# Float32 products of the attention, 64 output rows at a time on two halves of the TensorE array

## The chip, the cores and the metric

The kernel runs on one core of a Trainium2 chip. The metric is the device time of one execution in microseconds (us), taken from the first to the last work of the program. The kernel before takes 977.47 us, the median of three runs that lie between 977.23 and 977.64 us.

## The reference

A linear attention with random features (4 batches, 8 heads, 576 rows of 64 columns, 128 features), and behind it two feed-forward blocks of 512 x 2048 x 512 on the 2304 rows that come out:

```python
def phi(x):
    proj = np.einsum('bhsd,md->bhsm', x, omega)
    h = proj - np.sum(x * x, axis=-1, keepdims=True) / 2.0
    h = h - np.max(h, axis=-1, keepdims=True)
    return np.exp(h) / np.sqrt(m)
q_p, k_p = (phi(q_s), phi(k_s))              # q and k, scaled
kv = np.einsum('bhsm,bhsd->bhmd', k_p, v)
z = np.sum(k_p, axis=2)
num = np.einsum('bhsm,bhmd->bhsd', q_p, kv)
den = np.einsum('bhsm,bhm->bhs', q_p, z)[..., None] + 1e-06
x = num / den                                # then rows (b, s), columns (h, d)
x = relu(x @ w_in) ** 2 @ w_out              # first block
x = elu(x @ w_in2) @ w_out2                  # second block
```

The change touches the two products `kv` (phi(k) with v; a column of ones in v gives `z` in the same product) and `num` (phi(q) with `kv`, which gives `den` in its last column).

## The kernel before, in words

The 576 rows of a head are 4 blocks of 128 and 64 left over. A unit of work is a pair of heads of one batch, for k or for q (`(b, "k", hp)`, `(b, "q", hp)`), and one unit `(b, "l", 0)` holds the left-over rows of all eight heads. That makes 9 units a batch and 36 in all. A loop written out by hand runs over the units with `stages`, a table of steps and of the delay of each: squares, transposes (`transposed`, tile `pt`, line 275), projection with omega in three float32r products (`projected`, `pp`, line 292), maxima, exponentials (`featured`, `ph`, line 321), and then the steps that matter here, all in plain float32:

- `used`, for a k unit: for each of two heads, four products add phi(k) of a block, transposed by the product itself, times `v` of that block (128 rows by 65 columns) into `pk` (line 340). A ninth product adds the left-over rows of both heads (130 columns, line 344). ScalarE then copies `pk` to `kv` (line 348).
- `used`, for a q unit: transposes phi(q) to `qT` (tile `pq`, line 358).
- `attended`, for a q unit: for each of two heads, four products of a 128 x 128 block of `qT` with `kv` (65 columns) into `pn` (line 381). After every second pair of heads, four products for the left-over rows, which have 64 output rows only (`pl`, line 398). VectorE divides by the last column.
- `turned`: transposes the result for the feed-forward blocks (`px`, line 413, and `pxl`, line 422).

Each of the nine or eight products holds one operand in the array (the weights: phi(k) or `qT`, 128 rows by 128 columns) and streams the other (`v` or `kv`). A float32 product stands as two weight loads and two matmuls in the trace. The order of the instructions on TensorE is the order in which this loop issues them; `used` of a k unit and `attended` of the q unit before it stand right behind one another. In the last units, the first steps of the feed-forward blocks (`gemm1`, line 457; `gemm2`, line 508) are interleaved, and they fill the rest of the program.

Of the kernel before, what the change touches and what calls it, by code (L numbers as in the profile page):

```python
# [17 lines left out]
def linear_attention_two_ffn_kernel(  # L18
# [12 lines left out]
    nc = tc.nc  # L31
    P = 128
    B, H, S, D = q.shape
# [4 lines left out]
    C = S // P  # L38
# [10 lines left out]
    SCALE = float(D) ** -0.25  # L49
    HALF = 0.5 * SCALE * SCALE  # L50
    EPS = 1e-6 * M

    REBIAS = 2.0 ** -112
    assert LH * L == P and C == 4 and H == 4 * LH and 2 * NP * (C * P) == W * H and NP == KD
# [9 lines left out]
    def page(shape, name, dt=F32):  # L64
        return pages.tile([P] + list(shape), dt, tag="page", name=name)

    def psum(name):
        return ps.tile([P, W], F32, tag="bank", name=name)

    def flat(t):  # L70
        return t.rearrange("p a b -> p (a b)")
# [134 lines left out]
    st = {}  # L206
# [120 lines left out]
    def used(u):  # L327

        b, kind, hp = u
        nm = f"{b}{kind}{hp}"  # L330
        phs = st[u]["ph"]
        if kind == "k":
            ll = st[b, "l", 0]
            kv = sp.tile([P, 2, D + 1], F32, tag="kv", name=f"kv{nm}")
            pk = psum(f"pk{nm}")

            for h in range(2):
                o = pk[:, h * (D + 1):(h + 1) * (D + 1)]
                for c in range(C):
                    nc.tensor.matmul(  # L340
                        o, phs[h][:, c, :], st[u]["v"][:, h * C + c, :], start=h == 0 and c == 0, stop=False,
                        skip_group_check=True,
                    )
            nc.tensor.matmul(
                pk[:, :2 * (D + 1)], ll["ph"][0][:, hp, :], flat(ll["v"][:, 2 * hp:2 * hp + 2, :]),
                start=False, stop=True, skip_group_check=True,
            )
            nc.scalar.copy(out=flat(kv), in_=pk[:, :2 * (D + 1)])
            st[u]["kv"] = kv
            return  # L350
        st[u]["qT"] = []
        for g in range(2):
            if kind == "l" and g == 0:
                continue
            qT = page([4, P], f"qT{nm}_{g}")
            pt = psum(f"pq{nm}_{g}")
            for i in range(4):
                nc.tensor.transpose(pt[:, i * P:(i + 1) * P], phs[g][:, i, :], ident)
            nc.scalar.copy(out=flat(qT), in_=pt)
            st[u]["qT"].append(qT)  # L360

    def normal(pvs, os, w, nm):
        rd = sp.tile([P, 4 * len(pvs), 1], F32, tag="rd", name=f"rd{nm}")
        rds = [rd[:w, 4 * i:4 * i + 4] for i in range(len(pvs))]
        for pv, r in zip(pvs, rds):
            nc.vector.tensor_scalar(out=r, in0=pv[:, :, D:D + 1], scalar1=EPS, scalar2=None, op0=ALU.add)
        nc.vector.reciprocal(out=rd[:w], in_=rd[:w])
        for pv, o, r in zip(pvs, os, rds):
            nc.vector.tensor_tensor(out=o, in0=pv[:, :, :D], in1=r.to_broadcast([w, 4, D]), op=ALU.mult)

    def attended(u):

        b, kind, hp = u
        if kind != "q":
            return
        xs = page([C, 2, D], f"xs{b}_{hp}")
        pvs = []
        for h in range(2):
            pn = psum(f"pn{b}_{hp}_{h}")
            for c in range(C):  # L380
                nc.tensor.matmul(  # L381
                    pn[:, c * (D + 1):(c + 1) * (D + 1)], st[u]["qT"][h][:, c, :], st[b, "k", hp]["kv"][:, h, :],
                    start=True, stop=True,
                )
            pvs.append(pn[:, :C * (D + 1)].rearrange("p (c d) -> p c d", d=D + 1))
        normal(pvs, [xs[:, :, h, :] for h in range(2)], P, f"{b}_{hp}")
        st[u]["xs"] = xs
        if hp % 2 == 0:
            return
        qd = hp // 2  # L390
        if qd == 0:
            st[b, "xs"] = page([H, D], f"xsl{b}")
        xs = st[b, "xs"]
        qTl = st[b, "l", 0]["qT"][0]
        pn = psum(f"pl{b}_{qd}")
        for i in range(4):
            j, h = 2 * qd + i // 2, i % 2
            nc.tensor.matmul(  # L398
                pn[:L, i * (D + 1):(i + 1) * (D + 1)], qTl[:, j, h * L:(h + 1) * L],
                st[b, "k", j]["kv"][:, h, :], start=True, stop=True,  # L400
            )
        normal([pn[:L, :4 * (D + 1)].rearrange("p (c d) -> p c d", d=D + 1)], [xs[:L, 4 * qd:4 * qd + 4, :]], L, f"l{b}_{qd}")
# [151 lines left out]
    def moe_pieces():  # L554
# [14 lines left out]
    stages = (  # L569
        (transposed, 2), ("weights", 0), (featured, 4), ("step", 1), (projected, 3), (load, 0),  # L570
        (maxima, 3), (squared, 1), ("step", 0), (used, 5), (turned, 7), (attended, 6), (load_v, 2),
    )
    DEPTH = max(d for f, d in stages)
# [5 lines left out]
    with tc.manual_schedule():  # L579
# [4 lines left out]
        for s in range(1, len(units) + DEPTH):  # L584
# [21 lines left out]
            u = s - DEPTH  # L606
# [36 lines left out]
```

## Time and profile before

| | |
|---|---|
| time, median of three runs | 977.47 us |
| span of the profiled execution, from the first to the last instruction | 975.3 us |
| what lies around the span in a run, by the difference | 2.2 us |
| TensorE (PE) busy | 968.4 us, 99% |
| TensorE weight loads (PEld) busy, beside the matmuls | 837.1 us, 86% |
| VectorE (DVE) busy | 621.1 us, 64% |
| ScalarE (ACT) busy | 479.2 us, 49% |
| GpSimd (POOL) busy | 91.2 us, 9% |

Busy means that at least one instruction of the engine was recorded as running. A matmul is recorded from its start to the modelled end of its result, so the records of neighbouring matmuls overlap, and a matmul's recorded length (275 ns, say) is not what it takes from the next one. What it takes is read from the distance between starts, or from the chain of work, in which each piece counts up to where the next takes over.

### The profile page before, as it was taken

The numbers are of one execution on the slowest core, as the hardware profiler recorded it, in microseconds if no ns is written. First come the engines' busy times: TensorE is split into PE (matmuls) and PEld (weight loads), VectorE is DVE, ScalarE is ACT, GpSimd is POOL, SyncE is SP. The second block draws the span as 40 slices with busy tenths as digits, with TensorE's granted clock in tenths as the row PEclk, the third lists the DMA queues.
The fourth block names the chain that finished last, engine by engine and source line by source line (L and its number), as shares of the span: only waits on it lengthen the run. The fifth ranks groups of instructions, "written<-read, shape, count | busy, mean of one in ns | idle before, by whom it ended". The sixth has DMA issues, their size and how long they took to land.

```text
span 975.3 us, 14149 instructions
## 1 busy us (share of the span) xinstructions
PE 968.4 (99%) x5457; PEld 837.1 (86%) x5457; DVE 621.1 (64%) x1130; ACT 479.2 (49%) x1052; POOL 91.2 (9%) x196
## 2 busy tenths in 40 slices
PE   9999999999999999999999999999999999999998
PEld 9999999999888888888888888888888888888886
DVE  6888886574584358435764587558745884485444
ACT  6887885442352234223443366446544654454443
POOL 7455553000000000000000000000000000000000
PEclk9999999999999999999999999999999999999999
DMA  9355420020140013001210022003200220000211
GB/s 249 93 144 140 137 66 2 1 87 1 43 130 1 1 48 104 22 1 44 87 43 1 22 85 68 1 1 101 73 1 0 87 87 1 1 22 13 74 44 65
DMA packets 56610, 53.40 MB, mean 55 GB/s; under 512 B 25568, under 2 KB 50144, under 8 KB 56544
## 3 DMA queue, kind: packets, MB, share of 16 engines
q1 hardware_dynamic: 55696, 52.08, 17.7%
q8 instruction: 43, 0.70, 0.3%
q10 hardware_dynamic: 848, 0.43, 0.2%
q14 instruction: 23, 0.19, 0.1%
HBM read 47.78 MB, written 4.72 MB: 54 GB/s over the span
## 4 chain that ended last, share of the span: by engine, by line
PE 97%; DMA 1%; SPq 1%; ACT 1%; DVE 0%; issue 0%; ACTq 0%
PE ph L457 41%; PE py L508 41%; PE pn L381 3%; PE pk3k L340 1%; PE pk2k L340 1%; PE pk1k L340 1%; PE pk0k L340 1%; PE px L413 1%; PE pp3k L292 1%; PE pp1k L292 1%; PE pp3q L292 1%; PE pp0q L292 1%; PE pp1q L292 1%; DMA ld0k<-in_k_dram 1%; PE pl L398 1%; PE pp0k L292 0%
## 5 line engine op out<-in xcount | busy, mean ns | idle before, releaser
L457 PE MATMUL ph<-xh,wh 128*128 128x512 f32 (+1 forms) x688 | 245.7, 357 | 0.0
L457 PE MATMUL ph<-xl,wh 128*128 128x512 f32 (+1 forms) x688 | 245.7, 357 | 0.0
L457 PE MATMUL ph<-xh,wl 128*128 128x512 f32 (+1 forms) x688 | 245.7, 357 | 0.0
L469 ACT ACTIVATE r<-ph 128x512 f32<-128x512 f32 (+1 forms) x92 | 46.8, 509 | 241.1 <-PE ph L457 241.1
L473 DVE TENSOR_TENSOR gf<-r 128x512 f32<-128x512 f32 (+1 forms) x92 | 53.3, 579 | 154.5 <-ACT r L469 154.1
L457 PEld LDWEIGHTS ph<-xh,wh 128*128 128x128 f32 x688 | 129.3, 188 | 21.3 <-DVE gf L483 0.2
L457 PEld LDWEIGHTS ph<-xl,wh 128*128 128x128 f32 x688 | 129.3, 188 | 21.1
L457 PEld LDWEIGHTS ph<-xh,wl 128*128 128x128 f32 x688 | 129.3, 188 | 20.5
L74 DVE TENSOR_TENSOR gl<-gf,gh 128x512 fp32r<-128x512 f32 (+1 forms) x172 | 105.2, 611 | 47.3 <-ACT gh L484 35.5
L508 PE MATMUL py<-gh,wh 128*128 128x512 f32 (+1 forms) x368 | 127.4, 346 | 0.0
L508 PE MATMUL py<-gh,wl 128*128 128x512 f32 (+1 forms) x368 | 126.8, 345 | 0.0
L508 PE MATMUL py<-gl,wh 128*128 128x512 f32 (+1 forms) x368 | 126.7, 344 | 0.0
L482 DVE SCALAR_TENSOR_TENSOR r<-r,t 128x512 f32<-128x512 f32 (+1 forms) x80 | 51.0, 637 | 105.2 <-ACT t L479 105.2
L508 PE MATMUL py<-wh,gh 128*128 128x512 f32 x288 | 113.7, 395 | 0.0
L508 PE MATMUL py<-wh,gl 128*128 128x512 f32 x288 | 113.5, 394 | 0.0
L508 PE MATMUL py<-wl,gh 128*128 128x512 f32 x288 | 113.3, 393 | 0.0
L477 ACT ACTIVATE gf<-ph 128x512 f32<-128x512 f32 (+1 forms) x80 | 44.4, 555 | 93.5 <-PE ph L457 93.3
L484 ACT CAST gh<-gf 128x512 fp32r<-128x512 f32 (+1 forms) x80 | 46.2, 578 | 82.0 <-DVE gf L483 80.4
L508 PEld LDWEIGHTS py<-gh,wh 128*128 128x128 f32 x368 | 69.2, 188 | 9.4
L508 PEld LDWEIGHTS py<-gh,wl 128*128 128x128 f32 x368 | 69.2, 188 | 9.2
L508 PEld LDWEIGHTS py<-gl,wh 128*128 128x128 f32 x368 | 69.2, 188 | 9.0
L531 DVE TENSOR_TENSOR ya<-py,ya 128x512 f32<-128x512 f32 x108 | 67.2, 682 | 0.6 <-PE py L508 0.6
(325 smaller groups left out, 1460.6 us busy)
## 6 DMA issues: line engine op xcount, KB each, us to landing
st<-in_moe_w_in_dram SPq DMA_DIRECT2D x32, 512.0 KB, 3.6
st<-in_moe_w_out_dram SPq DMA_DIRECT2D x32, 512.0 KB, 3.4
vk<-in_v_dram SPq DMA_DIRECT2D x32, 128.0 KB, 4.2
out_dram<-ya SPq DMA_DIRECT2D x16, 256.0 KB, 2.2
ld0k<-in_k_dram SPq DMA_DIRECT2D x4, 256.0 KB, 4.8
ld0q<-in_q_dram SPq DMA_DIRECT2D x4, 256.0 KB, 4.8
ld1k<-in_k_dram SPq DMA_DIRECT2D x4, 256.0 KB, 4.6
ld1q<-in_q_dram SPq DMA_DIRECT2D x4, 256.0 KB, 4.2
```

Source lines behind the costliest of these rows:

```text
L74: eng.tensor_tensor(out=out, in0=whole, in1=hi.bitcast(F32), op=ALU.subtract)
L292: nc.tensor.matmul(pp[:, i * 2 * M:(i + 1) * 2 * M], a[:, cs], o, start=(n == 0), stop=(n == 2))
L340: nc.tensor.matmul(o, phs[h][:, c, :], st[u]["v"][:, h * C + c, :], start=h == 0 and c == 0, stop=False, skip_group_check=True,)
L381: nc.tensor.matmul(pn[:, c * (D + 1):(c + 1) * (D + 1)], st[u]["qT"][h][:, c, :], st[b, "k", hp]["kv"][:, h, :], start=True, stop=True,)
L457: nc.tensor.matmul(ph[:, :n], wt[:, cs], x_part(xt, moe, i, c)[:, n0:n1], start=(m == 0), stop=(m == 3 * KD - 1))
L469: nc.scalar.activation(out=r, in_=ph[:, :n], func=AF.Relu)
L473: nc.vector.tensor_tensor(out=gf, in0=r, in1=r, op=ALU.mult)
L477: nc.scalar.activation(out=gf, in_=ph[:, :n], func=AF.Relu, scale=-1.0)
L482: nc.vector.scalar_tensor_tensor(out=r, in0=r, scalar=1.0, in1=t, op0=ALU.add, op1=ALU.mult)
L484: nc.scalar.copy(out=gh, in_=gf)
L508: nc.tensor.matmul(y, *((w[:, ts], a) if moe == 0 else (a[:, ts], w)), start=j == 0 and m == 0 and t % per == 0, stop=j == GF - 1 and m == ...
L531: nc.vector.tensor_tensor(out=ya_t[i, t], in0=yv, in1=ya_t[i, t], op=ALU.add)
```

## The change

The weights of each product of lines 340, 344 and 381 are cut into two halves of 64 columns, and each half goes out as a product of its own, to output partitions 0 to 63 or 64 to 127 of the same bank. The two halves are issued alternately. What is computed, the buffers and the instructions on the other engines stay. In the built program such a product carries the array tile 128 rows x 64 columns, at column 0 or at column 64; lines 340, 344 and 381 carried 128 x 128 before, and line 398 carried 128 x 64 at column 0 already and still does.

```diff
+    HALVES = (slice(0, P // 2), slice(P // 2, P))
...
             for h in range(2):
-                o = pk[:, h * (D + 1):(h + 1) * (D + 1)]
                 for c in range(C):
-                    nc.tensor.matmul(
-                        o, phs[h][:, c, :], st[u]["v"][:, h * C + c, :], start=h == 0 and c == 0, stop=False,
-                        skip_group_check=True,
-                    )
-            nc.tensor.matmul(
-                pk[:, :2 * (D + 1)], ll["ph"][0][:, hp, :], flat(ll["v"][:, 2 * hp:2 * hp + 2, :]),
-                start=False, stop=True, skip_group_check=True,
-            )
+                    for m in HALVES:
+                        nc.tensor.matmul(
+                            pk[m, h * (D + 1):(h + 1) * (D + 1)], phs[h][:, c, m], st[u]["v"][:, h * C + c, :],
+                            start=h == 0 and c == 0, stop=False, skip_group_check=True,
+                        )
+            for m in HALVES:
+                nc.tensor.matmul(
+                    pk[m, :2 * (D + 1)], ll["ph"][0][:, hp, m], flat(ll["v"][:, 2 * hp:2 * hp + 2, :]),
+                    start=False, stop=True, skip_group_check=True,
+                )
...
             for c in range(C):
-                nc.tensor.matmul(
-                    pn[:, c * (D + 1):(c + 1) * (D + 1)], st[u]["qT"][h][:, c, :], st[b, "k", hp]["kv"][:, h, :],
-                    start=True, stop=True,
-                )
+                for m in HALVES:
+                    nc.tensor.matmul(
+                        pn[m, c * (D + 1):(c + 1) * (D + 1)], st[u]["qT"][h][:, c, m], st[b, "k", hp]["kv"][:, h, :],
+                        start=True, stop=True,
+                    )
```

TensorE's rows at the second k unit of the first batch, before. A row is a line, an operation, output and inputs, and the shape of the output; `pk` comes from `used`, `pn` from `attended` of the q unit before:

```order
L292 MATMUL pp0k_1_435<-oml,th0k_349 128x256
L340 MATMUL pk0k_457<-vk_106,ph0k_0_353 128x65 x4
L340 MATMUL pk0k_457<-vk_106,ph0k_1_358 128x65 x4
L344 MATMUL pk0k_457<-vl_112,ph0l_0_238 128x130
L381 MATMUL pn_0_0_469<-kv0k_276,qT0q_0_391 128x65 x4
L381 MATMUL pn_0_1_474<-kv0k_276,qT0q_1_398 128x65 x4
L275 MATMUL pt0k_485<-ident,ld0k_377 128x128 x4
```

The same place on TensorE in the changed program (its lines have shifted):

```order
L293 MATMUL pp0k_1_444<-oml,th0k_358 128x256
L341 MATMUL pk0k_466<-vk_106,ph0k_0_362 64x65 x8
L341 MATMUL pk0k_466<-vk_106,ph0k_1_367 64x65 x8
L346 MATMUL pk0k_466<-vl_112,ph0l_0_238 64x130 x2
L384 MATMUL pn_0_0_487<-kv0k_276,qT0q_0_400 64x65 x8
L384 MATMUL pn_0_1_496<-kv0k_276,qT0q_1_407 64x65 x8
L276 MATMUL pt0k_511<-ident,ld0k_386 128x128 x4
```

Nothing has moved; each product stands twice with half the output rows, between the same neighbours. There are 17 unbroken stretches of products with the 128 x 64 tile in the changed program, and 8 (those of line 398) in the one before.

## Rows read from the trace of the kernel before

**Rows 1.** The page: span, TensorE's busy time, the chain's shares by engine.

```profile
span 975.3 us, 14149 instructions
...
PE 968.4 (99%) x5457; PEld 837.1 (86%) x5457; DVE 621.1 (64%) x1130; ACT 479.2 (49%) x1052; POOL 91.2 (9%) x196
...
PE 97%; DMA 1%; SPq 1%; ACT 1%; DVE 0%; issue 0%; ACTq 0%
```

**Rows 2.** Chain of work, 10 to 60 us: start, us, what.

```profile
22.18 1.73 PE pk0k L340 x16
23.91 0.28 PE pk0k L344 x2
24.18 1.73 PE pn L381 x16
25.92 0.44 PE pt0k L275 x4
...
32.96 1.73 PE pn L381 x16
34.70 0.61 PE pl L398 x8
35.31 0.59 PE pt1k L275 x4
```

**Rows 3.** Busy time by stretch, instructions in brackets, granted TensorE clock, DMA.

```profile
core 0: us, PE busy (x) PEld busy (x) DVE busy (x) ACT busy (x) POOL busy (x), PEclk, DMA share, GB/s
13.00:33.00 20.00, 20.00 (x180) 20.00 (x178) 15.77 (x32) 19.56 (x64) 14.07 (x31) 1.00 0.84 235
...
13.00:133.00 120.00, 119.66 (x1061) 117.64 (x1059) 101.69 (x225) 102.39 (x322) 68.07 (x141) 1.00 0.49 136
133.00:190.00 57.00, 57.00 (x501) 56.36 (x501) 36.52 (x90) 33.31 (x101) 14.80 (x30) 1.00 0.07 20
```

**Rows 4.** TensorE by line and form: busy us, mean ns, idle before; first batch.

```profile
L381 PE MATMUL pn<-kv0k,qT0q 128*128 128x65 f32 x64 | 7.6, 272 | 0.0
L340 PE MATMUL pk0k<-vk,ph0k 128*128 128x65 f32 x64 | 7.6, 272 | 0.0
L344 PE MATMUL pk0k<-vl,ph0l 128*128 128x130 f32 x8 | 1.8, 302 | 0.0
L398 PE MATMUL pl<-kv0k,qT0l 128*64 128x65 f32 x16 | 1.4, 228 | 0.0
```

**Rows 5.** Weight loads in order of time (start, us, what), three short windows.

```profile
32.69 1.87 PEld L381 LDWEIGHTS pn<-kv0k,qT0q 128*128 128x128 f32 x16
34.62 0.54 PEld L398 LDWEIGHTS pl<-kv0k,qT0l 128*64 128x64 f32 x8
...
25.36 0.41 PEld L381 LDWEIGHTS pn<-kv0k,qT0q 128*128 128x128 f32 x3
```

**Rows 6.** Matmuls in order of time, beside the last row of the group above.

```profile
25.42 0.39 PE L381 MATMUL pn<-kv0k,qT0q 128*128 128x65 f32 x2
```

**Rows 7.** Lines 340 and 381: duration min/median/max, first and last start.

```profile
L340 PE MATMUL pk3k<-vk,ph3k x64: 218/275/275, 129.3 to 177.8; 128*128 128x65 f32 x64
...
L381 PE MATMUL pn<-kv2k,qT2q x64: 221/275/275, 103.7 to 132.9; 128*128 128x65 f32 x64
```

**Rows 8.** ScalarE's waits, 13 to 133 us: total, times, longest.

```profile
ACT th2q L278 <- PE pt2q L275: 3.4, 2, 2.7
ACT th1q L278 <- PE pt1q L275: 2.9, 2, 2.1
ACT th2k L278 <- PE pt2k L275: 2.7, 1, 2.7
...
ACT th0k L278 <- PE pt0k L275: 0.4, 1, 0.4
```

## The prediction, made before the changed kernel was run

> **What bounds the kernel now.** I read the page first: TensorE is busy for 99% of the span and holds 97% of the chain that ended last [rows 1]. The list of TensorE's groups then shows no idle time ahead of the lines that change [rows 4], and by stretches TensorE is busy for 119.66 of the 120 us from 13 to 133 us and for all of the 57 us up to 190 us, at the full granted clock of 1.00, its level of 2.4 GHz [rows 3]. So a nanosecond less on TensorE ends the program a nanosecond earlier, as long as no other engine comes to be late. Two are near in the first stretch: VectorE has 101.69 us of work there and ScalarE 102.39; ScalarE is busy for 19.56 of the 20 us from 13 to 33 us [rows 3]. Behind 133 us both have much room.
>
> What do the changed lines take? Recorded durations overlap, so I take the chain in order of time [rows 2]: the eight products of a k unit take 1.73 us (16 pairs of load and matmul), the ninth 0.28, the eight of a q unit 1.73. There are 16 k units and 16 q units with one such group each (4 batches, 4 pairs of heads): 16 x (1.73 + 0.28 + 1.73) = **59.8 us**, all of it on the path.
>
> What limits such a product? Sixteen loads of 128 columns cover 1.87 us, the last of them 0.19 long by itself, so they start (1.87 - 0.19)/15 = 112 ns apart; the loads of line 398, half as wide and followed by matmuls of the same 65 columns, start (0.54 - 0.14)/7 = 57 ns apart, 0.14 being the length of one of these [rows 5]. Half the columns, half the distance: the pace is set by the weight load, not by the 65 columns that stream. The 130 columns of line 344 take 0.28 for two, hardly more than two of the others, and say the same [rows 2].
>
> **The change part by part.** (a) The 512 pairs of lines 340 and 381 become 1024 with half the load, the 32 pairs of line 344 become 64. What one takes in the new order, with the two halves of the array in turns, no row shows: line 398 uses one half alone. I bound it from both sides. Lowest: the halves work fully side by side, and two pairs take the 57 ns of one in line 398, 28.5 ns each. That gives 1024 x 28.5 ns = 29.2 us and 64 x 57 ns = 3.6 us (twice the columns), 32.8 us. Next: a load starts when the matmul before it has started, but a matmul on a half that stands empty need not wait for its whole load. In line 381 a load starts at 25.36 and its matmul at 25.42, 56 ns into the 112 [rows 5, 6]; at half the width that is 28 ns for the first pair of a half and 57 for the second, 42.5 on average: 43.5 us, and with some 70 ns for the wide ones 4.5 more, 48.0 us. Highest with the overlap missing: 57.5 ns each, as in line 398, which is the first rival.
>
> I take 36 ns, the middle of 28.5 and 42.5, since nothing in the rows chooses between free loads and loads in step: 36.9 us, and 64 x 60 ns = 3.8 us, together **40.7 us**.
>
> The Trainium skill (TensorEngine Tiling (Array Packing), section Key Properties) says that different tiles of the array can execute weight loads and matmuls in parallel. By that alone the sum would be the 32.8 us of the lowest bound; no run here shows it yet.
>
> (b) Entering and leaving the 128 x 64 tile costs something. Line 398 shows it: its eight pairs take 0.61 in the chain where 8 x 57 ns are 0.46, and the transposes behind it take 0.59, where they take 0.44 behind line 381 [rows 2]: 0.15 + 0.15 = 0.30 us for each stretch. There are 17 stretches instead of 8 (the products of a k unit, a q unit and line 398 now share one): 9 x 0.30 = **2.7 us** more.
>
> (c) Nothing else is added: no wait, no DMA, no work on another engine. ScalarE's copy of `pk` and VectorE's first read of `pn` wait for the last of the products as before, and get it earlier if these are faster.
>
> Sum on TensorE: 40.7 + 2.7 - 59.8 = -16.4 us.
>
> (d) How much of it reaches the end? The first three batches and the first k group of the fourth lie before 133 us (line 340 of batch 3 begins at 129.3, line 381 of batch 2 ends at 132.9) [rows 7]: 13 + 12 of 32 groups, so 12.8 of the 16.4 us. The stretch of 120 us would become 107 us, with ScalarE busy for 102.4 and VectorE for 101.7 of them. Of ScalarE's 17.6 us of idle time, 14.6 end with a transpose of TensorE (seven rows from 3.4 down to 0.4) [rows 8], so they do shrink when TensorE is earlier; but at 95% of occupation each jitter costs, and from 13 to 33 us ScalarE has nothing left to give. I count two thirds, 8.5 us. Behind 133 us VectorE and ScalarE have 20 us of room, and the other 3.6 us count whole. Together 12.1 us. The profiled execution's span is 975.3 us, with 2.2 us around it that do not change: 975.3 + 2.2 - 12.1 = **965.4 us**, against the median of 977.47.
>
> The two ends of this case: at 42.5 ns the sum is 48.0 + 2.7 - 59.8 = -9.1 us, of which 7.1 x 2/3 + 2.0 = 6.7 arrive: 970.8 us. At 28.5 ns it is -24.3 us; 19.0 fall before 133 us, and two thirds of these and all of the rest make 18.0: 959.5 us. Were ScalarE's idle time used to the last (17.6 + 5.3), 954.6 us.
>
> **The rivals.** *The halves don't overlap* (the change doesn't do what it says): each half-load waits its turn, 57.5 ns as in line 398. For it speaks that in every stream of this trace the loads come one behind another, at a distance that goes by their columns [rows 5]. Against it, that all these streams use a single tile, so that no load had anywhere else to go. Price: 1024 x 57.5 = 58.9 us, the wide ones 64 x 57.5 = 3.7 us, or 64 x 110 = 7.0 us if the 130 columns now count (a transpose of 128 columns takes 0.44/4 = 110 ns [rows 2]); with 2.7 for the stretches and less 59.8 that is +5.5 to +8.8 us, all on the path: 983 to 986.3 us, **985**. It decides from 52.5 ns a pair on: there 1088 pairs and 2.7 us make the old 59.8.
>
> *The turns hold the loads up*: a load for one half can't start while a matmul of the other still streams. Then at each change of halves the 57 ns of streaming and a load of 28 to 57 stand one behind the other, and the second pair adds 57: 71 to 85 ns a pair, 72.7 to 87 us, with some 6.5 for the wide ones and 2.7 for the stretches +22 to +36 us: 1000 to 1014 us. The even pace of line 398, where a load runs beside the matmul of its own tile [rows 5], speaks against it. The Trainium skill (TensorE: Matmul & The Clock Gate, Part 3, The mechanism) has the rule behind it: loads overlap with matmuls in flight only when the row group differs, and two column halves share all rows. Line 398 already breaks that rule in its own tile.
>
> *The gain is swallowed*: TensorE saves as forecast, but ScalarE and VectorE make the first 133 us as long as before, by their own order of work. Then only the last 7 of 32 groups count, 2 to 5 us: 972 to 975.5 us. The 14.6 us of idle time that TensorE ends speak against it.
>
> *A pace close to break-even*, 50 to 54 ns, would end within 2 us of before.
>
> **How the numbers follow.** Overlap with a gain that arrives (954.6 to 970.8): 0.52. Swallowed: 0.07. Break-even: 0.05. No overlap, 985: 0.28. Held up, over 1000: 0.08. Faster is 0.52 + 0.07 = 0.59, the same 0.05 (0.2%, 2 us, is about what a measurement of this kernel can tell from no change), slower 0.36. The range must take in the case without overlap; it runs from 955 to 987 and leaves out the held-up turns and a sliver at either end. The likeliest case alone has 955 to 971.
>
> **What would show it.** The distance between the starts of loads in lines 341 and 384 of the changed kernel: near 28 to 43 ns the forecast's step (a) holds, 57 is the first rival, over 70 the second. The eight products of a k unit, 1.73 us in the chain, should take about 1.15. The transposes behind each stretch should take 0.59, as behind line 398, which tests (b). For (d): the length up to the end of line 384, ScalarE's idle time behind `pt`, and any new idle time of TensorE in front of lines 293 and 341. Granted clock below 1.00 in the first stretch would make the prediction wrong in a way not counted here.

## The result, and the profile after

The changed kernel takes **963.42 us** (963.22 to 963.81, four runs) against 977.36 us for the kernel before on the same chip: ratio 0.9856, with a 95% interval of 0.9842 to 0.987, 13.9 us less. The forecast was 965.4 us in a range of 955 to 987. Of all the runs below, one execution of `quarters` took 1005.06 us at a mean granted clock of 0.882; the trace of `quarters` is of that execution, its time in the table the median of all four.

The weight loads in order of time, at one k group and the q group behind it, beside [rows 5] of before (start, us, what):

```profile
30.14 1.01 PEld L341 LDWEIGHTS pk0k<-vk,ph0k 128*64 128x64 f32 x32
31.07 0.20 PEld L346 LDWEIGHTS pk0k<-vl,ph0l 128*64 128x64 f32 x4
31.23 1.07 PEld L384 LDWEIGHTS pn<-kv0k,qT0q 128*64 128x64 f32 x32
32.22 0.55 PEld L401 LDWEIGHTS pl<-kv0k,qT0l 128*64 128x64 f32 x8
```

Thirty-two loads cover 1.01 us, one of them 0.14, so they start (1.01 - 0.14)/31 = 28 ns apart on average. The eight of line 401, which stay on one half, still start (0.55 - 0.14)/7 = 59 ns apart. So the two halves work side by side, and two pairs take the time of one.

The same stretch in the chain of work, beside [rows 2]:

```profile
30.21 1.08 PE pk0k L341 x32
31.29 0.22 PE pk0k L346 x4
31.51 0.93 PE pn L384 x32
32.45 0.46 PE pl L401 x8
32.90 0.60 PE pt1k L276 x4
```

1.73 + 0.28 + 1.73 = 3.74 us has become 1.08 + 0.22 + 0.93 = 2.23. The entry into the 128 x 64 tile is now in the 1.08 and no longer in line 401 (0.46 instead of 0.61), and the transposes behind it take 0.60 where they took 0.44. With 16 groups, eight uses of line 401 and nine more ends of a stretch, TensorE has 16 x 1.51 + 8 x 0.15 - 9 x 0.16 = **23.9 us** less to do. Only 13.9 arrive.

Where the others stay is told by the stretches of time (busy us, instructions in brackets, clock, DMA), which answer to [rows 3]; 13 to 126 us now ends where 13 to 135 us did, at the first feed-forward product:

```profile
13.00:33.00 20.00, 19.81 (x290) 18.49 (x289) 16.15 (x32) 19.91 (x66) 14.57 (x31) 1.00 0.85 236
...
13.00:126.00 113.00, 108.03 (x1513) 100.44 (x1511) 103.83 (x230) 103.56 (x326) 69.28 (x144) 1.00 0.55 148
126.00:180.00 54.00, 52.93 (x621) 51.46 (x622) 38.85 (x92) 33.18 (x102) 13.48 (x28) 1.00 0.05 14
```

TensorE was busy for all but 0.34 of 120 us; now 5 of 113 are open. A busy matmul is recorded up to its modelled end, so its weight loads tell more: they leave 12.6 of the 113 us open (113.00 - 100.44), where they left 2.4 of 120 [rows 3]. VectorE and ScalarE do 104 us in 113, 92%. The page's share of the chain says the same: TensorE holds 88% of it instead of 97%, and VectorE 7%:

```profile
span 962.0 us, 15238 instructions
...
PE 88%; DVE 7%; ACT 3%; DMA 1%; issue 1%; SPq 0%; POOL 0%; ACTq 0%; POOLq 0%
```

And ScalarE's waits, 13 to 126 us (total, times, longest), beside [rows 8]:

```profile
ACT ph2q L322 <- POOL nb2q L312: 2.4, 3, 1.6
ACT ph2k L322 <- POOL nb2k L312: 1.1, 1, 1.1
ACT ph1k L322 <- POOL nb1k L312: 1.0, 2, 0.6
...
ACT th2k L279 <- PE pt2k L276: 0.7, 1, 0.7
```

The waits for TensorE's transposes, 14.6 us before, have shrunk to some 2.7. In their place ScalarE waits for the bias of the exponentials: `nb` comes from three small steps on GpSimd behind VectorE's maxima, and these waits add up to 6.8 us (six rows, 2.4 to 0.7) where they were 1.7. TensorE itself now waits too, 13 to 180 us (four of nine rows; `xs` is VectorE's division behind the attention, `xl` one of its subtractions ahead of the feed-forward products):

```profile
PE pq2l L360 <- DVE xs L371: 0.9, 1, 0.9
PE ph L460 <- DVE xs L371: 0.9, 1, 0.9
PE pp2q L293 <- ACT ph2q L322: 0.9, 1, 0.9
PE ph L460 <- DVE xl L75: 0.8, 1, 0.8
```

In all it waits 3.4 us for VectorE and 2.1 for ScalarE's exponentials; before, the only such row was one of 0.3 us. So the other engines' work has become as long as TensorE's in this stretch.

### The profile page after: what moved, and what is told of

It is laid out like the page before. It is cut to its first block, busy times and chain, and to the rows that moved or that the text cites. A ratio compares the mean times of both kernels' runs of the same rounds, so it can differ in the third digit from the quotient of the medians.

```text
span 962.0 us, 15238 instructions
## 1 busy us (share of the span) xinstructions
PE 948.9 (99%) x6001; PEld 811.6 (84%) x6001; DVE 622.9 (65%) x1130; ACT 479.2 (50%) x1052; POOL 91.0 (9%) x196
## 4 chain that ended last, share of the span: by engine, by line
PE 88%; DVE 7%; ACT 3%; DMA 1%; issue 1%; SPq 0%; POOL 0%; ACTq 0%; POOLq 0%
PE ph L460 42%; PE py L511 42%; DVE xl L75 1%; ACT ph0q L322 1%; PE pn L384 1%; DVE xs L371 1%; DVE cv L131 0%; PE pp3q L293 0%; ACT ph0k L322 0%; DVE cv L140 0%; DMA ld0l<-in_k_dram 0%; ACT ph1k L322 0%; DVE wl L75 0%; DVE mx1q L306 0%; PE pq3q L360 0%
```

## The experiments

All times are medians; 977.11, 976.96, 977.26 and 977.36 us are those of the kernel before in the four sets.

| run | us | against before | 95% interval |
|---|---|---|---|
| the change | 963.42 | 0.9856 | 0.9842 to 0.987 |
| no_turns | 967.1 | 0.9898 | 0.9883 to 0.9913 |
| pk_only | 971.0 | 0.9938 | 0.9923 to 0.9953 |
| pn_only | 969.0 | 0.9917 | 0.99 to 0.9933 |
| quarters | 965.0 | 0.9875 | 0.9859 to 0.9892 |
| light_before | 976.43 | 0.9995 | 0.9985 to 1.0004 |
| light_after | 952.41 | 0.9748 | 0.9734 to 0.9763 |
| act_light_after | 960.84 | 0.9834 | 0.982 to 0.9849 |
| dve_light_after | 956.04 | 0.9788 | 0.9774 to 0.9803 |
| early_26 | 966.85 | 0.989 | 0.9875 to 0.9904 |
| early_26_before | 982.07 | 1.0062 | 1.0042 to 1.0082 |
| low_on_pool | 959.16 | 0.9814 | 0.98 to 0.9829 |
| high_low_on_pool | 960.31 | 0.9819 | 0.9795 to 0.9842 |

The theory after the result: the halves overlap fully, TensorE saves some 24 us, and other engines take up ten of them in the first 126 us. The rival: TensorE itself saves no more than the 14 us that are seen.

### Is it the turns?

The two loops change places, in `used` and in `attended` alike:

```diff
-                for c in range(C):
-                    for m in HALVES:
+                for m in HALVES:
+                    for c in range(C):
```

> Same halves and the same number of products as in the changed kernel, but for each head all four products of the first half go out ahead of the four of the second. Theory (two halves run side by side only where neighbours in the order are of different halves): the pace goes back to 57 ns a pair, TensorE takes 5 to 9 us more than before the change, less what overlaps at the few seams: about 980 us, between 976 and 986. Rival (TensorE looks far enough ahead to pair the halves by itself): as the changed kernel, 963 us.

Measured: 967.1 us, 3.7 more than with the turns and far from 980. The theory on the turns fell; the rival is nearly right. The loads in order of time show how (start, us, what):

```profile
30.21 0.60 PEld L341 LDWEIGHTS pk0k<-vk,ph0k 128*64 128x64 f32 x12
```

In program order a head has eight pairs for the first half and eight for the second. These twelve loads start within 0.60 - 0.14 = 0.46 us, 42 ns apart, where loads of one half alone are 57 to 59 ns apart. The chain at the same place as above:

```profile
30.23 1.30 PE pk0k L341 x29
31.53 0.06 PE pk0k L346
31.59 0.06 PE pk0k L341
31.65 0.16 PE pk0k L346 x2
...
33.08 0.29 PE pl L401 x5
33.37 0.59 PE pt1k L276 x4
```

And two rows of its matmuls in order of their starts:

```profile
31.32 0.33 PE L346 MATMUL pk0k<-vl,ph0l 128*64 128x130 f32 x1
31.37 0.28 PE L341 MATMUL pk0k<-vk,ph0k 128*64 128x65 f32 x2
```

A matmul of line 346 starts at 31.32 us, ahead of three of line 341 (31.37 us and later) that stand before it in the program. So TensorE does not keep to the order of the program here, neither for its loads nor for its matmuls. The trace doesn't name the half of a product; that it starts ahead what a free half can take is the reading that fits the rows. From the start of the k group to the transposes it takes 33.37 - 30.23 = 3.14 us, against 32.90 - 30.21 = 2.69 with the turns and 35.31 - 30.95 = 4.36 before (the 30.95 is where line 340 begins in the chain that [rows 2] are from). Without turns 73% of the saving on TensorE is left: the turns bring the rest.

### The k and the q products alone

pk_only leaves line 381 of the kernel before as it was (its edit to the changed kernel stands here), pn_only in the same way lines 340 and 344:

```diff
-                for m in HALVES:
-                    nc.tensor.matmul(
-                        pn[m, c * (D + 1):(c + 1) * (D + 1)], st[u]["qT"][h][:, c, m], st[b, "k", hp]["kv"][:, h, :],
+                nc.tensor.matmul(
+                    pn[:, c * (D + 1):(c + 1) * (D + 1)], st[u]["qT"][h][:, c, :], st[b, "k", hp]["kv"][:, h, :],
...
```

> Only the products with v are in halves, those with phi(q) whole. TensorE saves some 11 us on these lines and pays a change of tile behind each of 16 k groups, 2.4 us: 8.7 us less work. Theory (the changed kernel's TensorE saves some 23 us and other engines take up the part that does not arrive, the last part of it first): most of the 8.7 us arrives, 969 to 971 us. Rival (the part that does not arrive was never saved on TensorE): about 14/23 of it, 972 us or later.

> Only the products of phi(q) are in halves. TensorE saves some 12 us on line 384, pays for entering the tile 16 times and leaving it 8 times more, 3.4 us, and saves 1.6 on line 398, which is then entered from the same tile: 10 us less. Theory (others absorb the last part first): 968 to 970 us, and the two savings of this run and of the one with the k products alone add up to more than the 13.9 us of the whole change. Rival (TensorE itself saves only 14): 971 us or later, and the two add up to less than 13.9.

Measured: 971.0 and 969.0 us, 6.1 and 8.1 us less than before. Both lie in the theory's ranges, the first at the upper end, and together they are 14.2 us, a little over the 13.9 of the whole; within the intervals this is no more than equal, so the pair speaks for the theory but does not settle it. The chain of pn_only shows the price of a change of tile between groups:

```profile
31.49 1.73 PE pk0k L341 x16
33.22 0.28 PE pk0k L345 x2
33.50 1.08 PE pn L383 x32
34.58 0.46 PE pl L400 x8
```

Line 383 takes 1.08 us where it takes 0.93 in the whole change: the entry, 0.15 us, is paid here. In pk_only the k group pays it, and ahead of the whole products behind it the loads stand still for 0.17 us (in brackets: idle before):

```profile
31.48 1.86 PEld L383 LDWEIGHTS pn<-kv0k,qT0q 128*128 128x128 f32 x16 [0.17 <-issue]
```

### Does TensorE really save 24 us?

The squares and maxima go, and one exponential without bias does the work of four (phi without its shift), in the kernel before and in the changed one:

```diff
...
-            for i in range(4):
-                nc.scalar.activation(
-                    out=ph[:, i, :], in_=pp[:, i * M:(i + 1) * M], func=AF.Exp,
-                    bias=nb[:, 4 * g + i:4 * g + i + 1],
-                )
+            nc.scalar.activation(out=flat(ph), in_=pp, func=AF.Exp)
...
-        (maxima, 3), (squared, 1), ("step", 0), (used, 5), (turned, 7), (attended, 6), (load_v, 2),
+        ("step", 0), (used, 5), (turned, 7), (attended, 6), (load_v, 2),
```

> The kernel before, with work taken off the other engines: the squares and maxima are left out and the exponentials have no bias, so that one instruction does four of them (phi without its shift). TensorE's work is the same. The change is bound by TensorE before, so this is little faster: 974 to 977 us in either theory.

> The changed kernel with the same work left out (squares, maxima, the bias of the exponentials). Theory (TensorE saves some 23 us and ScalarE, VectorE and GpSimd take up 10 of them): now nearly all of it arrives, 22 to 24 us less than the light version of before, 951 to 955 us. Rival (TensorE saves no more than 14): 13 to 15 us less, 961 to 963 us.

Measured: 976.43 and 952.41 us. With the other engines out of the way the change is worth **24.0 us**, what the chain's pieces give (23.9), and without the change the same relief is worth nothing that can be told from zero. The rival has fallen. In the stretch up to the first feed-forward product of light_after, TensorE has no idle time again, and its loads leave 3.2 us open:

```profile
13.00:116.50 103.50, 103.50 (x1518) 100.27 (x1517) 61.87 (x151) 74.97 (x156) 0.00 (x0) 1.00 0.60 164
```

### Which engine takes it up?

act_light_after has the edit of the exponentials alone. dve_light_after leaves out squares and maxima alone and gives the exponentials a zero bias:

```diff
...
-        nb = st[u].pop("nb")
+        nb = no_bias
...
```

> The changed kernel with ScalarE alone relieved: exponentials without bias, one instruction for four (phi without its shift; the maxima are still worked out and not used). If ScalarE alone takes up the missing 10 us, 953 to 956 us; if VectorE does as much, little changes: 960 to 963 us.

> The changed kernel with VectorE and GpSimd relieved: squares and maxima left out, the bias of the exponentials is zero, ScalarE's work as it was. If VectorE alone takes up the missing 10 us, 953 to 956 us; if ScalarE does as much, 960 to 963 us. Where both are in turn the last, each of the two runs gains a part, and neither the whole.

Measured: 960.84 and 956.04 us, 2.6 and 7.4 us less than the change, of 11.0 that both bring (the kernel before took 0.4 us less in this set than in that of the change). VectorE with the GpSimd steps behind it is the greater part, ScalarE the smaller; the two add up to 10.0. In act_light_after VectorE is busy for 106 of 110 us, in dve_light_after ScalarE for 102 of 107:

```profile
13.00:123.30 110.30, 104.39 (x1511) 99.39 (x1509) 106.10 (x231) 77.15 (x155) 69.26 (x143) 1.00 0.55 152
```

```profile
13.00:119.60 106.60, 105.29 (x1515) 100.34 (x1515) 61.06 (x151) 102.10 (x324) 0.00 (x0) 1.00 0.58 157
```

The first row is act_light_after, the second dve_light_after. VectorE and GpSimd were relieved together. TensorE's own waits name VectorE: in act_light_after, 13 to 180 us, these are all of them, 5.8 us for the division alone:

```profile
PE pq2q L356 <- DVE xs L367: 2.2, 2, 1.7
PE pq2l L356 <- DVE xs L367: 1.8, 1, 1.8
PE ph L456 <- DVE xs L367: 1.8, 1, 1.8
```

In dve_light_after 1.2 us of waits are left, and in light_after none. This speaks for VectorE over GpSimd, but no run here relieves GpSimd alone.

### Four quarters

```diff
-    HALVES = (slice(0, P // 2), slice(P // 2, P))
+    HALVES = tuple(slice(i, i + P // 4) for i in range(0, P, P // 4))
```

> Four quarters of 32 columns instead of two halves. Theory (with two halves the 65 streamed columns last as long as a half load, so they are the limit from here on): four quarters start every 57 ns, TensorE's work does not change, 962 to 966 us. Rival (the loads are still the limit): pairs of quarters at half the distance again, 15 us less on TensorE, of which half arrives: 955 us.

Measured: 965.0 us, 1.6 more than with halves. The time alone would not settle it, as the other engines take up part of any saving on TensorE. The loads do, in order of time (start, us, what); the last row is the stretch around them by engine, at a granted clock of 0.85:

```profile
30.80 1.03 PEld L341 LDWEIGHTS pk0k<-vk,ph0k 128*32 128x32 f32 x64
33.19 0.56 PEld L401 LDWEIGHTS pl<-kv0k,qT0l 128*64 128x64 f32 x8
...
30.00:34.00 4.00, 4.00 (x153) 3.67 (x153) 3.59 (x10) 3.27 (x11) 3.23 (x8) 0.85 0.97 302
```

Sixty-four loads, one of them 0.11, start (1.03 - 0.11)/63 = 15 ns apart, four in 58 ns. The eight of line 401 on one half start (0.56 - 0.14)/7 = 60 ns apart in the same trace. A quarter has half the columns to load and still takes as long for a pair as a half, so the loads are no longer the limit, as the theory said. That the streamed columns are shows in the change itself: line 346, with 130 of them behind the same half loads, takes 0.22/4 = 55 ns a pair, against 0.93/32 = 29 ns in line 384 with 65.

### Can the gain be had?

Two ways. early_26 fills TensorE's new idle time with feed-forward work; early_26_before is its control.

```diff
-    WEIGHTS, THREE, FIRST, TWO = 4, 18, 33, 34
+    WEIGHTS, THREE, FIRST, TWO = 4, 18, 26, 34
```

> The changed kernel with the first steps of the feed-forward block started at loop pass 26 instead of 33, one a pass: seven pieces of 12 matmuls with 256 columns, 7 x 12 x 118 ns = 9.9 us of TensorE's work, go into the stretch in which TensorE now waits for VectorE and ScalarE. They bring about 4 us of VectorE's work along. Theory (TensorE idles there for about 10 us, and VectorE is the engine that holds it up): 4 to 6 us come back, 957 to 960 us. Rival (the passes are so tightly coupled that the added VectorE work pushes everything by as much): 962 to 965 us.

> The same earlier start in the kernel before. There TensorE has no idle time in that stretch, so in either theory nothing is gained: 976 to 979 us. A gain here of several us would say that the earlier start has a merit of its own and does not show where the change's gain went.

Measured: 966.85 us, 3.4 more than the change, and 982.07 us, 4.8 more than before. Neither theory had a loss in the control: the earlier start has a price of its own in both. In early_26 it shows in the stretches of two us around 104 us (columns as above):

```profile
100.00:102.00 2.00, 1.36 (x12) 1.15 (x10) 1.91 (x3) 2.00 (x7) 1.88 (x2) 1.00 0.83 229
102.00:104.00 2.00, 0.51 (x5) 0.54 (x6) 1.93 (x7) 1.94 (x7) 0.00 (x0) 1.00 1.00 236
104.00:106.00 2.00, 2.00 (x14) 1.99 (x12) 2.00 (x5) 0.00 (x0) 0.29 (x2) 0.58 0.59 155
106.00:108.00 2.00, 2.00 (x12) 2.00 (x11) 1.97 (x4) 0.50 (x1) 1.92 (x3) 0.57 0.68 167
```

TensorE stands still for most of two us, and after that the granted clock is 0.58 and 0.57, a mixture of its two levels of 1.2 and 2.4 GHz. At a mean granted clock of 0.999 the same program took 965.0 us, at 0.996 it took 966.8 to 966.9, so some 1.9 of the 3.4 us go with the clock. The waits name VectorE's `xs` ahead of a transpose and of a feed-forward product, 2.1 and 1.9 us. The other way takes work from VectorE:

```diff
-        minus(nc.vector, l, tf, h)
+        minus(nc.gpsimd if n < 2 * GF else nc.vector, l, tf, h)
```

> The changed kernel with the low parts of the first eight weight pieces subtracted on GpSimd instead of VectorE: 8 x 0.7 us less on VectorE up to about 126 us, 8 x 1 us more on GpSimd. Theory (VectorE is the main one that takes up the gain): 2 to 4 us back, 959 to 962 us. Rival (GpSimd's own small steps ahead of the exponentials come later for it, and ScalarE waits): no gain, 963 us or later.

Measured: **959.16 us**, 4.3 less than the change and 18.1 less than before, a little more than the 2 to 4 of the theory. VectorE has 99.5 instead of 103.8 us in a stretch that is now 109.8 long:

```profile
13.00:122.80 109.80, 107.36 (x1511) 100.19 (x1510) 99.47 (x225) 103.13 (x323) 77.64 (x148) 1.00 0.55 150
```

GpSimd takes 1.5 us for each of the eight subtractions, not the 1 us of the expectation, and still ScalarE's waits for the bias fall, from 6.8 to 3.4 us. This speaks for VectorE's work, more than GpSimd's, as what held the bias up. The same move in the kernel before was not run; light_before says that relieving VectorE is worth nothing there.

Giving GpSimd the high parts as well (the float32r copy of the same eight pieces, from ScalarE) was the last step:

```diff
-        nc.scalar.copy(out=h, in_=tf)
+        if n < 2 * GF:
+            nc.gpsimd.tensor_copy(out=h, in_=tf)
+        else:
+            nc.scalar.copy(out=h, in_=tf)
```

> As the version with the low parts on GpSimd, and the high parts of the first eight weight pieces (8 x 0.7 us) go from ScalarE to GpSimd too, which is busy for 77 of 109 us there and gets some 8 us more. If ScalarE, with 102 of 109 us, is the last now: 1 to 3 us more, 956 to 958 us. If GpSimd's queue delays the bias of the exponentials by as much: 959 to 961 us. Floor by the relieved versions: about 953 us.

Measured: 960.31 us, 1.2 more (the intervals of the two ratios overlap). Its ScalarE waits for GpSimd's bias are longer (three of seven rows):

```profile
ACT ph2k L325 <- POOL nb2k L315: 2.6, 3, 1.1
ACT ph2q L325 <- POOL nb2q L315: 1.7, 3, 1.0
ACT ph1k L325 <- POOL nb1k L315: 1.5, 2, 1.0
```

They add up to 7.6 us against 3.4 in low_on_pool, while ScalarE's busy time up to 122.8 us falls by 3.3, from 103.1 to 99.8: what ScalarE is spared it spends waiting. low_on_pool is the fastest of the versions that leave nothing of the reference out.

## Why the prediction was right, step by step

*What bounds the kernel*: right. TensorE's saving of 23.9 us is told by the chain's pieces, and in the light pair, with the other engines out of the way, 24.0 arrive.

*(a) The pace of a pair*: right in kind, too careful in size. 36 ns was put between 28.5 and 42.5; 28 ns were measured, the lower end. The rule that a load follows the start of the matmul before it, which gave the upper end, was read from streams on a single tile; across two, 28 ns a pair leave no room for it. (The lengths of single loads that the working subtracts, 0.19 and 0.14, stand in no row of [rows 5]; the trace has 192 and 138 ns as their medians.) The sign set for this step, 1.15 us for a k group, left out the entry of step (b): the 1.08 measured are 0.93 and 0.15, so it came closer than the pace did. The sum on TensorE was -16.4 us and came to -23.9; with the lower end it was -24.3, right within half a microsecond. This is the term that was mis-sized most.

*(b) The stretches*: right. 0.15 us at entry and 0.16 at the end were seen in line 341 and in the transposes, as line 398 had shown.

*(c) Nothing else is added*: right for the instructions, not for the waits. ScalarE's for the bias grew from 1.7 to 6.8 us, and TensorE, which had waited 0.3 us for another engine, waited 5.5.

*(d) How much arrives*: two thirds were forecast up to 133 us and all behind it. The first feed-forward product, behind 25 of the 32 groups, begins with its load at 126.3 us instead of 135.5:

```profile
L457 PEld LDWEIGHTS ph<-xh,wh x688: 186/188/195, 135.5 to 965.6; 128*128 128x128 f32 x172
...
L460 PEld LDWEIGHTS ph<-xh,wh x688: 186/188/195, 126.3 to 952.4; 128*128 128x128 f32 x172
```

So 9.2 us had arrived there, of 16 x 1.51 x 25/32 = 18.9 us saved on the 25 groups: one half. The remaining 4 to 5 us arrived behind it, nearly whole as forecast. Both engines were named, and both have a part; that VectorE and the GpSimd steps behind it would weigh more, with no more work on VectorE than on ScalarE in [rows 3], was not foreseen.

So the closeness of the time, 965.4 against 963.42, is in part luck, since two errors of size ran against each other: 7.5 us too little saved on TensorE, and too large a part of the saving taken to arrive. From the pace measured, the working's own lower end of 959.5 us would have been the forecast, 4 us too fast.

*The rivals*: the halves that don't overlap (985) fell with the 28 ns. The held-up turns, 71 ns a pair or more, fell with them. One line of the Trainium skill (TensorE: Matmul & The Clock Gate, Part 3, The mechanism) has loads overlap with matmuls in flight only where the row group differs. This trace does not agree with that line: both halves share all rows, and loads run beside the other half's matmuls. What the Trainium skill says in TensorEngine Tiling (Array Packing), Key Properties, that tiles execute loads and matmuls in parallel, the trace bears out, with 28 ns a pair against 57. The swallowed gain held in part: ten of 24 us.

## What to carry to other kernels

Short float32 products (65 streamed columns behind a load of 128) are bound by the weight load, which shows when a load of half the columns halves the distance between starts; cut into two column halves in turns, they ran at nearly twice the pace here (1.73 to 0.93 us for eight), for 0.3 us at each stretch in the other tile. Four quarters brought nothing more. Before counting such a saving, add up the other engines' busy time in the same stretch and look at who waits for whom behind them: here they stood at 85% of it, and half of what was saved in that stretch did not arrive. A version with those engines relieved, run with and without the change, prices that loss in one pair of runs.

## What the runs showed of the hardware that was not expected

- TensorE started matmuls out of program order: without turns a matmul of line 346 came ahead of one of line 341, and 967.1 us are only 3.7 us more than with the turns.
- Two halves take the time of one: 32 loads of 64 columns begin 28 ns apart, while 8 on a single half begin 59 ns apart. Four quarters take it too: 64 loads of 32 columns begin 15 ns apart.
- After TensorE had been busy for only 0.51 of 2 us, the granted clock fell to 0.58 for the next stretch (early_26, 102 to 106 us).
